# A written-out job order for an attention and MLP kernel, replaced by another with four changes of tiling fewer

## The chip, the cores and the metric

The kernel runs on one core of a Trainium2 chip. The time is that of one launch on the device, in microseconds (us); the median over several runs is given. A core has TensorE (PE, the matrix unit, whose weight loads the profile shows apart as PEld), VectorE (DVE), ScalarE (ACT), GpSimd (POOL) and SyncE (SP, which here only issues transfers). Each of them works through its own queue in order, and they wait for each other through semaphores. Matmuls write to PSUM, which has eight banks of 128 x 512 floats.

## The reference

One input x of 2048 tokens by 512 features is normalized once, and two branches are added to it:

```python
xn  = layernorm(x)
out = x + A(xn) + B(xn)
# A: attention, 32 heads of 16, in 4 segments of 512 tokens one after the other:
#    logits = q k^T * scale + mask (causal), p = softmax(logits), a_dot = p v
#    a_mem  = phi(q) M / (phi(q) z + 1e-6)      M, z: memory of the earlier segments
#    o      = g * a_mem + (1 - g) * a_dot       g = sigmoid(beta), one for each head
#    M += phi(k)^T v,  z += sum of phi(k);  phi(t) = t + 1 if t > 0 else exp(t)
#    A = concat(o) wo
# B: gelu(layernorm(xn) w1 + b1) w2 + b2       512 -> 1792 -> 512
```

## The kernel before, in words

The work is cut into 1308 jobs, and the order of the jobs is written out by hand as a string (ORDER, line 98), one letter a job. A letter names one of 39 streams (line 58); each stream is a list of jobs in a fixed order of its own, and the letter takes the next one of its stream. The function plan (line 130) walks through the string, and the kernel's last loop (line 896) calls the function of each job, which puts its instructions on the queues of all engines at once. So the string sets the order of every engine's queue and of the transfers too: on each engine the instructions stand in the order of the jobs, and an instruction waits until the data that it reads and the buffer that it writes are free. A second string (BANKS, line 115) gives the PSUM bank of each accumulation tile in the order in which they are asked for (line 160).

Matrix products of 512-long sums are made with float16 halves: each operand is a high and a low part, and three products are added (split3, line 483). Weights are therefore loaded, squared and summed for a scale, scaled and split in the kernel itself.

The attention works in 16 groups i = 4 s + g, segment s (512 tokens) and head group g (8 heads). The jobs that matter here, with the letters of the string:

- a: X, load, statistics and scaling of 256 tokens, and Xt, their transposition. b: ratio. f: zeros and constants. u: warm, eight matmuls without use that fill the start.
- g and h: T(i, 1) for keys and T(i, 0) for queries (line 515): twelve matmuls, a copy by ScalarE and one by VectorE, three writes to device memory on SP's queue (lines 528 to 530), and, when both of a group are there, four reads that bring them back in another layout as kst and qst (line 536).
- i: N, the transposed keys. j: M(i, n), the maximum over the logits, n from 0 to 11, two or four matmuls with an eviction by VectorE each (lines 638 and 645), and R(i), which turns the maxima, sends them through memory and adds them to qst (lines 651 to 661).
- k: S(i, t, n), logits and exponentials (lines 678 and 683) and GpSimd's selects (line 692). l: pv and PV, the sums over values (line 707). m: O, normalization. n: K, the memory's update (line 619), and Z, Qd and Q, its use. o: V(s, b), the values (line 604), copied by ScalarE (line 610).
- p: D(j, f), the first MLP product for 256 tokens and half of the 1792 columns, seven in a set (line 771). q: G and H, gelu and the split. r: e(j, n), the second MLP product, six matmuls each, fourteen in a set (line 814). s: out, the product with wo (line 832). t: A(tok, 0), the load of x into an accumulator tile by SP (line 793), and A(tok, 1), the add of b2 to it by a transfer that GpSimd issues (line 797).
- v to D: the weights' loads (wl), and E to M: their squares (wm), scales (wf) and splits (ws). "1a" and "1b" are the first and second half of w1, "2a" and "2b" those of w2; qk, QK and RK are the head groups 0, 1 and 2 with 3 of wk and wq. The squares of 1a are made by TensorE (line 315), those of 1b by ScalarE (line 308), and wf adds them up by matmuls with ones (lines 349 and 351).

TensorE's array is used in three tilings: whole (T, V, D, out, warm and the weights' sums), in two halves of 64 rows (e, M, S, R, N, Qd and the later transpositions), and in four strips of 32 columns (pv, PV, K). Where two jobs that follow each other differ in it, the tiling changes. ScalarE changes its function table for gelu and back, 16 times each.

## Time and profile before

| what | value |
|---|---|
| median of 3 runs | 695.29 us (694.94 to 695.43) |
| profiled execution, its own time | 700.17 us |
| span of the profile | 698.5 us |
| TensorE busy | 684.0 us |
| VectorE, ScalarE, GpSimd busy | 542.7, 503.8, 340.4 us |
| granted TensorE clock, mean | 0.995 |

The profile shows one execution. Its span runs from the first to the last recorded instruction; the execution's own time is 1.7 us longer. A row of the timeline merges instructions of one line that follow each other: start, busy time, engine and line, what it writes and reads, its shape and how many. The busy time of a matmul reaches to its modelled end, so rows overlap, and the distance between starts tells the work better. In brackets stands idle time before the row and what ended it. A row of the waits gives who waited for whom, the sum in us, how often, and the longest. A row of the windows gives the busy time of the engines in a stretch, and behind them TensorE's granted clock, the share of the DMA engines that was busy, and GB/s. A row of the DMA issues names what is moved, the queue, how many and KB each.

### The profile page before, as it was taken

To read this page: it belongs to the slowest core of one execution; us is meant where nothing else is said; L and a number is where in the kernel's file an instruction comes from. 1 tells how busy PE (TensorE), PEld (TensorE's weight loads), DVE (VectorE), ACT (ScalarE), POOL (GpSimd) and SP (SyncE) were. 2 spreads that over 40 slices of the span, in tenths; PEclk is the share of its full clock that TensorE was granted. 3 is DMA by queue.
4 is the path that set the end of the run, shared out by engine and by line. 5 is a ranking of instruction groups with operands and counts; after the bars stand their busy time and mean duration, and the time that the engine had idled before them with its cause. 6 is when DMAs were issued, how large, how long until landed. Compare 5 with 4: busy or idle time off the path is not lost.

```text
span 698.5 us, 17165 instructions
## 1 busy us (share of the span) xinstructions
PE 684.0 (98%) x6465; PEld 396.0 (57%) x6465; DVE 542.7 (78%) x1740; ACT 503.8 (72%) x972; POOL 340.4 (49%) x526
## 2 busy tenths in 40 slices
PE   8999999999999999989999999999999999999997
PEld 6754656565644556555554556567464456556543
DVE  5988967997877967878687787988768588969432
ACT  4466898798786669647884787766876586877970
POOL 5235567365532634535324455355444335565752
PEclk9999999999999999999999999999999999999999
DMA  9986022411404131412123223051130404140101
GB/s 261 290 247 170 18 60 66 107 48 26 115 3 122 47 81 44 96 43 62 40 55 92 92 71 99 8 117 31 24 87 25 130 17 137 33 106 2 20 1 60
DMA packets 51791, 55.13 MB, mean 79 GB/s; under 512 B 4782, under 2 KB 40636, under 8 KB 51708
## 3 DMA queue, kind: packets, MB, share of 16 engines
q1 hardware_dynamic: 49404, 49.84, 24.8%
q0 software_dynamic: 2304, 4.20, 3.6%
q8 instruction: 50, 0.82, 0.5%
q14 instruction: 33, 0.27, 0.1%
HBM read 36.99 MB, written 17.04 MB: 77 GB/s over the span
## 4 chain that ended last, share of the span: by engine, by line
PE 84%; DMA 7%; ACT 3%; DVE 2%; SPq 1%; issue 1%; POOL 0%; DVEq 0%; ACTq 0%
PE ps L489 33%; PE ps L814 20%; PE ps L707 9%; PE ps L832 6%; PE ps L678 5%; PE ps L638 5%; DMA qd<-hl 2%; DMA qst<-qd 2%; PE ps L580 1%; PE ps L508 1%; DMA w1s<-in_B_w_dram 1%; ACT pt L683 1%; DMA oT<-in_B_w_dram 1%; DMA wqs<-in_A_wq_dram 1%; PE ps L845 1%
## 5 line engine op out<-in xcount | busy, mean ns | idle before, releaser
L645 DVE CUSTOM_DVE_ANT_0 ps<-ps,mask 128x512 f32<-128x512 f32 (+3 forms) x512 | 234.7, 523 | 17.6 <-PE ps L638 14.9
L683 ACT ACTIVATE pt<-ps,qkcs 128x512 f32<-128x512 f32 (+1 forms) x384 | 208.3, 621 | 52.9 <-PE ps L678 49.3
L814 PE MATMUL ps<-w2s,hT 64*128 64x512 f16 x1344 | 175.8, 377 | 0.6 <-DVE acc L820 0.5
L489 PE MATMUL ps<-xnT,w1s 128*128 128x256 f16 x1344 | 158.4, 273 | 0.0
L692 POOL TENSOR_SCALAR_AFFINE_SELECT pt<-pt 128x256 f32<-128x256 f32 x256 | 101.2, 415 | 95.2 <-ACT pt L683 93.9
L489 PEld LDWEIGHTS <-w1s 128*128 128x128 f16 x1344 | 127.7, 98 | 29.0 <-issue 11.0
L789 POOL TENSOR_TENSOR hT<-hh,hT 128x512 f16<-128x512 f32 x64 | 68.1, 1064 | 94.5 <-ACT hT L788 94.5
L814 PEld LDWEIGHTS <-hT 64*128 64x128 f16 x1344 | 71.7, 94 | 54.9 <-issue 4.5
L707 PE MATMUL ps<-pt,vt 128*32 128x512 f32 (+3 forms) x1024 | 76.0, 435 | 0.1
L773 DVE SCALAR_TENSOR_TENSOR hT<-ps,sc,sr 128x256 f32<-128x256 f32 x112 | 51.9, 478 | 27.2 <-PE ps L489 26.6
L645 DVE DVE_READ_ACCUMULATOR2_ANT mc<- 128x1 f32 x512 | 71.6, 140 | 0.1
L638 PE MATMUL ps<-kst,qst 48*128 48x512 f16 (+3 forms) x512 | 66.6, 298 | 2.9 <-DMA qst<-qd 2.3
L678 PE MATMUL ps<-qst,kst 50*128 50x512 f16 (+3 forms) x512 | 66.6, 298 | 1.8 <-DMA qst<-md 0.9
L788 ACT ACTIVATE hT<-hh 128x512 f16<-128x512 f32 x64 | 36.6, 573 | 27.7 <-POOL hh L787 27.2
L707 PEld LDWEIGHTS ps<-pt,vt 128*32 128x32 f32 x1024 | 31.1, 109 | 41.2 <-issue 32.2
L787 POOL TENSOR_SCALAR hh<-hT,sc 128x512 f32<-128x512 f32 x64 | 42.0, 656 | 23.1 <-ACT hT L780 20.8
L780 ACT ACTIVATE hT<-hT,b1t 128x256 f32<-128x256 f32 x112 | 46.7, 495 | 2.0 <-DVE hT L773 1.8
L489 PE MATMUL ps<-wvs,xnT 128*128 128x512 f16 x192 | 45.7, 390 | 0.0
L737 POOL TENSOR_TENSOR nN<-nN,oT 128x512 f32<-128x512 f32 x16 | 20.3, 1267 | 51.2 <-DVE oT L555 51.2
L678 PEld LDWEIGHTS <-kst 50*128 50x128 f16 x512 | 27.1, 94 | 31.2 <-issue 14.5
L489 PE MATMUL ps<-xnT,wqs 128*128 128x512 f16 x192 | 44.2, 380 | 0.0
L638 PEld LDWEIGHTS <-qst 48*128 48x128 f16 x512 | 28.1, 95 | 28.4 <-issue 9.3
(225 smaller groups left out, 909.9 us busy)
## 6 DMA issues: line engine op xcount, KB each, us to landing
kd<-hl SPq DMA_DIRECT2D x48, 128.0 KB
qd<-hl SPq DMA_DIRECT2D x48, 128.0 KB
kst<-kd SPq DMA_DIRECT2D x32, 192.0 KB
qst<-qd SPq DMA_DIRECT2D x32, 192.0 KB
acc<-in_A_x_dram SPq DMA_DIRECT2D x16, 256.0 KB
acc<-in_B_b_dram POOLq DMA_DIRECT2D x16, 256.0 KB, 4.1
out_dram<-acc SPq DMA_DIRECT2D x16, 256.0 KB
xt<-in_A_x_dram SPq DMA_DIRECT2D x14, 256.0 KB
```

What stands on the lines that cost most here:

```text
L489: T.matmul(p, wsl(ws, k, a), xsl(xs, k, b), start=s0 and i == 0, stop=s1 and i == 3 * n - 1)
L638: T.matmul(p[:, o:o + n], stk[i, 0][r, t, P * qb:P * qb + P], stk[i, 1][r, t, :n], start=True, stop=True)
L645: V.tensor_tensor_reduce(p[:, o:o + n], p[:, o:o + n], mask[:, 512 - n:], 1.0, -3e38, OP.add, OP.max, mc[:, 16 * b + 4 * t + qb:16 * b + 4 ...
L678: T.matmul(p[:, o:o + n], stk[i, 1][r, t, P * kb:P * kb + P], stk[i, 0][r, t, P * kb:], start=True, stop=True)
L683: A.activation(e[:, OFF[kbs[0]]:OFF[kbs[0]] + o], p[:, :o], AF.Exp, scale=qkcs[:, 1, i % NG:i % NG + 1])
L692: G.affine_select(v, v, pattern=[[0, 2], [1, P]], compare_op=OP.is_ge, fill=0.0, base=0, channel_multiplier=-1)
L707: T.matmul(p[32 * c:32 * c + 32, P * kb:], vt[s, kb][:, 4 * g + c, 16 * odd:16 * odd + 32], pt[i, 2 * c + odd][:, OFF[kb]:OFF[kb] + LEN[kb ...
L773: V.scalar_tensor_tensor(hz[:, fi, :], p[:, :256], col(F1 + fh), srow[hs][:, own], op0=OP.mult, op1=OP.mult)
L780: A.activation(z, z, AF.Gelu_apprx_tanh, bias=b1t[:, FH * (j % 2) + f:FH * (j % 2) + f + 1])
L787: G.tensor_scalar(t, hz[:, z, :], col(SHH + j % 2), 0.0, op0=OP.mult, op1=OP.add)
L789: G.tensor_tensor(hT[:, z, 1, :], t, hT[:, z, 0, :], op=OP.subtract)
L814: w = T.matmul(pes[j][a], hTs[fh][r, fi, u, P * a:P * a + P], w2s[r, fo, v, :], start=n == 0 and m == 0, stop=fi == FH - 1 and m == 2, ski ...
```

## The change

All code stays. The two strings are replaced: ORDER has the same letters in another order, so that the streams' own orders stand, and BANKS has other banks to fit. By its description the new order makes 225 changes of tiling in place of 229 and is one that allows for late loads and for GpSimd's transfers beside the queue's.

```diff
 ORDER = (
-    "auauvfdcauufaExauuEaGxaGwEbyfaFFGyEaEGGuAzuFzegHHJHauFGJuGHiAHHhCHFIIBtHpHHppHIJppIpJpBjjqBJIIgjIqjtoKCIIoujqjK"
-    "jKKhKIJojqLqjoLjrjjrrrnJKLDrDjijKrjppKMLKJLtkJrkpkjrkjrjKJrkpkjpKjMLjllllpKkjtrjkpkjkrjLrLkLkgjnlLlLqltluhqppkL"
...
+    "aufauucvafauaxuEdwuxEGayFEbayuFGEaaGuAeGzEzFGguHHGJHufFiHAHHhHIJIHpHpJHGIpHJFIppppIjjIBqjBqBgIJKoItIqKKoKujjjCC"
+    "hIKLjqjjLoLoDJKjajrrjnKrrqLrjijtrJjpKpKJLJkrkkpkjrKjrtjkpJpkjrtjKKjltlllpjkrLjkpkjkrjrLLkkgjLllLntqllhppqLrkLDk"
...
 )
 BANKS = (
-    "012531714607252301476502431056712645213076407541623037541231607543273410265734012654012654061254065421065421056"
...
+    "307127514306527014705325621740356523475160172345670124345762013561047235612043715620415642015625401642501654201"
...
 )
```

What this does at the places of which the prediction speaks:

- Start. Before, warm jobs 8 and 9 both stand behind the squares of 1a; now warm 8 stands ahead of them. The loads of v's second part and of QK change places.
- Second halves of w1 and w2. Before, the loads were issued in the order 2b first part, 1b first part, A(0, 0), 1b second and third part, T(1, 1)'s writes, 2b second part. Now it is the three parts of 1b, T(1, 1)'s writes, A(0, 0), and both parts of 2b. The squares of 1b stand before or around V(0, 1) instead of from V(0, 0) to T(1, 0); its wf job stays behind T(1, 0). The load of the next tokens (X(1, 0, 0)) moves from the start to M(0, 9).
- Group 7, from T(7, 0) to M(7, 0), jobs in order. Before: H e e e e M A(6, 1) e M M e G e M e H e M D D R M(7, 0). Now: e H e G e M e e e M e H M e e M M D H D R(6) A(6, 0) e M(7, 0), and A(6, 1) follows later, ahead of the first S of group 6.
- Group 15. Before: A(15, 0) PV M(15, 0) M(15, 1). Now: PV M(15, 0) S M(15, 1), and A(15, 0) later.
- Group 13. The last e job of set 11 now stands before T(14, 1) instead of behind it, and Z(14) before S(13, 0, 1).
- V(1, 3) moves from ahead of D(5, 0) to four short jobs ahead of K(4).
- A(tok, 0) and A(tok, 1) of most tiles change places against the other jobs; for tiles 9, 11 and 12 the two now stand close together.

## The prediction

> **What bounds the kernel now.** I read the page first, then the chain of work that ended last, then TensorE's own waits, and then the timeline of TensorE and of the queues around each of those waits.

> ```profile
> span 698.5 us, 17165 instructions
> PE 684.0 (98%) x6465; PEld 396.0 (57%) x6465; DVE 542.7 (78%) x1740; ACT 503.8 (72%) x972; POOL 340.4 (49%) x526
> ```

> TensorE is busy for 684.0 of 698.5 us, so it sets the time, and since the change adds and removes no matmul, only three things can move the end: the changes of tiling, the 14.5 us in which TensorE is idle, and stretches in which it is busy at a lower clock. In the timeline (columns: start us, busy us, engine and instruction, then in brackets the idle time before it and what ended it) the work of one job is the distance from its start to the next job's start:

> ```profile
> 104.50 0.81 PE L814 MATMUL ps<-w2s,hT 64*128 64x512 f16 x6
> 105.24 4.11 PE L489 MATMUL ps<-xnT,w1s 128*128 128x256 f16 x36
> 109.28 0.72 PE L678 MATMUL ps<-qst,kst 50*128 50x256 f16 x8
> ...
> 112.78 0.38 PE L638 MATMUL ps<-kst,qst 48*128 48x512 f16 x2
> 113.00 1.46 PE L814 MATMUL ps<-w2s,hT 64*128 64x512 f16 x12
> 114.29 0.49 PE L638 MATMUL ps<-kst,qst 48*128 48x384 f16 x6
> ```

> Two e jobs followed by a job of their own tiling (113.00 to 114.29) take 1.29 us, 0.645 each; one e followed by a D job, which uses the whole array, takes 0.74. A change of tiling is thus worth about 0.095 us. Three D jobs and one change take 4.04, so a D is (4.04 - 0.095) / 3 = 1.315. An M job of two matmuls takes 0.22.

> The two costliest places are these. The first is the scale of the second half of w1 (the wf job of "1b", lines 349 and 351) and the V job behind it; the first two rows show the same kind of job undisturbed, with six matmuls instead of ten, the windows show TensorE's granted clock as the third number from the right:

> ```profile
> 24.81 0.50 PE L349 MATMUL ps<-am,ones 128*128 128x1 f32 x4
> ...
> 25.47 0.46 PE L508 MATMUL ps<-ident,phk 64*128 64x64 f32 x8
> ...
> 53.46 0.28 PE L349 MATMUL ps<-am,ones 128*128 128x1 f32 x2
> 54.52 0.38 PE L349 MATMUL ps<-am,ones 128*128 128x1 f32 x2 [0.78 <-ACT w1s L308]
> ...
> 56.50 4.44 PE L489 MATMUL ps<-wvs,xnT 128*128 128x512 f16 x12
> ...
> 61.30 2.76 PE L489 MATMUL ps<-wvs,xnT 128*128 128x512 f16 x12
> ```

> ```profile
> 57.00:61.00 4.00, 4.00 (x13) 1.43 (x13) 2.28 (x8) 0.20 (x2) 0.00 (x0) 0.59 0.61 173
> 300.00:310.00 10.00, 8.40 (x61) 4.03 (x62) 6.40 (x25) 4.80 (x9) 2.27 (x2) 0.83 0.07 22
> ```

> Six such matmuls take 0.66 undisturbed, so ten would take 1.1; they took 56.50 - 53.46 = 3.04. That is 1.9 us of waiting, and then the V job takes 4.44 instead of 2.76, because the clock stood at 0.59: 1.7 us more. The second place is the first M job of head group 7:

> ```profile
> 292.28 0.58 SPq L530 DMA_DIRECT2D qd<-hl  x1
> 292.43 0.88 POOL L797 DMA_DIRECT2D acc<-in_B_b_dram  x1
> ...
> 297.70 1.25 SPq L536 DMA_DIRECT2D qst<-qd  x2
> ...
> 299.53 0.26 PE L508 MATMUL ps<-ident,mc 64*96 64x64 f32 x2
> 301.49 0.89 PE L638 MATMUL ps<-kst,qst 48*128 48x512 f16 x2 [1.70 <-DMA qst<-qd]
> ```

> TensorE stands still from about 299.6 to 301.49, 1.9 us, and the window 300 to 310 then has a mean clock of 0.83: 17% of 10 us, 1.7 us. So an idle gap here is paid about twice.

> **The change part by part.** Nothing but two strings changes: the order of the jobs on all engines, and the PSUM banks that go with it. I decoded both orders by the streams function and added up, with the prices above, the TensorE work that stands between each producer and its consumer (its cover).

> Tilings: by the shapes of the tiles I count 227 and 223, four fewer as stated, and by net count three of the four are steps from a row-tiled to a whole-array job, like the e and D above: 4 x 0.095 = 0.4 us. All of it is on the path, since TensorE is the path. Bounds 0.2 to 0.5.

> Start: one warm-up job is moved from behind the squares of w1's first half to just ahead of them.

> ```profile
> 21.16 1.61 PE L315 MATMUL ps<-w1s 128*128 128x128 bf16 x25 [0.79 <-DMA w1s<-in_B_w_dram]
> ...
> 22.84 1.03 PE L845 MATMUL ps<-ones 128*128 128x256 f16 x8
> 23.71 0.39 PE L315 MATMUL ps<-pt 128*128 128x128 bf16 x4
> ```

> A warm-up takes 23.71 - 22.84 = 0.87, and it now fills the 0.79 us in which TensorE waited for that load, which other loads of the same total size precede as before. Gain 0.8, bounds 0 (if an earlier stage of the start is late instead; the squares of the second q and k group now stand nearer to their load) and 0.9.

> Second half of w1: its squares on ScalarE waited for the load.

> ```profile
> 50.24 1.48 ACT L308 ACTIVATE w1s<-w1s 128x1536 bf16<-128x1536 f32 x1 [2.79 <-DMA w1s<-in_B_w_dram]
> ...
> 35.74 0.45 SPq L276 DMA_DIRECT2D w2s<-in_B_w_dram  x1
> 36.23 1.38 SPq L273 DMA_DIRECT2D w1s<-in_B_w_dram  x2
> 37.65 3.70 SPq L793 DMA_DIRECT2D acc<-in_A_x_dram  x1
> 41.40 3.88 SPq L273 DMA_DIRECT2D w1s<-in_B_w_dram  x2
> ```

> ```profile
> w2s<-in_B_w_dram SPq DMA_DIRECT2D x1, 1280.0 KB
> w1s<-in_B_w_dram SPq DMA_DIRECT2D x4, 320.0 KB
> ```

> On SP's queue 1280 KB of w2 and an acc tile stand ahead of or between these loads; in the new order both stand behind all of them. The 1280 KB are as much as the four w1 loads together, and the issues at 37.65 and 41.40 take 3.7 and 3.9 us, which tells of a full queue. From 35.7 to 50.2 some 2.8 MB moved, 5 us per MB: without the 1.5 MB the load lands several us earlier. The squares also stand about 3 us earlier in ScalarE's order. I take the whole wait and the slow clock as gone: 1.9 + 1.7 = 3.6, bounds 0 and 3.6.

> Group 7: in the order before, the add of b2 (line 797, issued by GpSimd) falls on the write and read of group 7's queries; in the new order it comes behind the first M. What remains is shown by group 14, with no such transfer:

> ```profile
> 584.44 0.57 SPq L530 DMA_DIRECT2D qd<-hl  x1
> ...
> 587.91 0.79 SPq L536 DMA_DIRECT2D qst<-qd  x2
> ...
> 592.09 0.69 PE L638 MATMUL ps<-kst,qst 48*128 48x512 f16 x6
> ```

> There 3.5 us pass from the last write's issue to the read's, against 5.4 in group 7, and 7.65 to the first M. Added to 292.28 this gives 299.9, where TensorE was at 299.6. The new order also has one e job more between the projection and the first M (ten for nine; five M, two D and R as before): 0.645 us. The cover grows so from 9.7 to 10.3 (nine e 5.8, five M 0.9, two D 2.6, changes and R 0.4), and the smallest over all groups from 8.8 to 10.0. The wait goes, and the slow clock with it: 1.9 + 1.7 = 3.6, bounds 0 and 3.9.

> [...]

> Two smaller waits:

> ```profile
> 587.30 0.70 PE L678 MATMUL ps<-qst,kst 50*128 50x256 f16 x7 [0.84 <-DVE hT L773]
> ...
> 628.88 0.55 PE L638 MATMUL ps<-kst,qst 48*128 48x512 f16 x4 [0.63 <-DMA qst<-qd]
> ```

> The jobs around the first are regrouped (the e pair's two evictions on VectorE come earlier); around the second an S job now stands between the first and second M, 0.2 us. I take 0.5 off for each, bounds 0 and 0.8, 0 and 1.3.

> What becomes thinner: the last V of the second segment stands 0.6 us before the K job that reads it (6.9 before), and ScalarE must copy it in between:

> ```profile
> 60.97 0.60 ACT L610 ACTIVATE vt<-ps 128x512 f32<-128x512 f32 x1 [3.80 <-PE ps L489]
> ```

> With 0.60 for the copy K, and with it all of TensorE's queue, waits 0.1 if ScalarE is free, 1 to 2 if it is behind. V to K of group 0 falls from 3.3 to 2.0, and M to R of groups 0 and 15 to some 2.4. The covers of the banks are alike in both orders. Three adds of b2 (tiles 9, 11, 12) now stand within 1 us of the load that they need, and GpSimd waits there with its selects for the S jobs queued behind it; the one such wait before was 0.9 us:

> ```profile
> POOL acc L797 <- DMA acc<-in_A_x_dram: 0.9, 1, 0.9
> ```

> The smallest cover from such an S to its reader is 1.6 us in both orders. With what I can't see I put 2.0 on this, bounds 0 and 6.

> Sum on the profiled execution: -0.4 - 0.8 - 3.6 - 3.6 - 1.0 + 2.0 = -7.4. Its own time is 700.17 and the median of the runs 695.29, 4.9 less with the same work, so some of the waits must be smaller when nothing is recorded. Idle 14.5 plus 3.4 of slow clock is 17.9; if the 4.9 lies there, 13/17.9 = 0.73 remains. Then the gain is 0.4 + 0.73 x 7.0 = 5.5, and the median 695.3 - 5.5 = 689.8. All good bounds and no new wait: 0.4 + 0.73 x 10.9 = 8.4, or unscaled 11.4.

> **The rivals.** (1) The waits removed belong to the recorded execution alone: the 4.9 us between profile and median are just these. Then 0.4 and the start are left and the thinner covers take them back: 694.8, no change. For it speaks that the two dips and gaps sum to 7.2; against it, that the load order and the 9.7 us of cover in group 7 are there in every run. (2) The clock dips come by themselves: 689.8 + 0.73 x 3.4 = 692.3. The two dips right behind the two longest waits speak against it. [...] (3) The collision moves: GpSimd's add now falls between R of group 6 and its first S, whose cover is 4.9 us by the count; a wait like group 7's of 1.9, with the clock, takes 3.6 x 0.73 = 2.6 back: 692.4. (4) Slower: the second half of w2 is now loaded last, behind group 1's keys, and its squares stand in ScalarE's order ahead of the copies of V that K of group 0 needs. At 5 us per MB its 2 MB take 10 us from about 45 and land near 55, ScalarE gets there at about 53. Beyond 2 us of lateness (the cover of V to K) each us is TensorE's, and from 1.5 us of gap on the clock adds 1.7. If the load takes 10 us longer than this, 8 + 1.7 us come on top of 689.8: 699.5. It decides against the change from some 6 us on. For it speaks that issues on SP took up to 3.9 us in this stage; against it, that less is queued then.

> **How the numbers follow.** A measurement of this kernel can tell about 0.2%, 1.4 us, from no change: 693.9 and 696.7 are the bounds. The forecast, 689.8, has 0.52; rival 1 has 0.14, rival 2 0.08, rival 3 0.12, rival 4 0.14. Faster by over 0.2%: 0.52 + 0.08 + 0.12 = 0.72. Within: 0.14. Slower: 0.14. The range runs from 685.0 (between the scaled and unscaled good ends, 686.9 and 683.9) to 695.0 (rival 1); left out are rival 4 and a few in a hundred below.

> **What would show it.** In the changed profile: no idle before line 349 at the second half of w1, the V job behind it 2.8 long and a clock of 1.0 to 65 us (load step); group 7's first M without a wait for qst, the write to read distance near 3.5 (collision step); the squares of w1's first half without the wait (start). The forecast is wrong if TensorE's idle time and slow clock stay near 17.9 in total, if a wait of over 1.5 us appears at K of group 0, S of group 6 or elsewhere, or if the median moves while these stay.

## The result, and the profile after

| what | before | after |
|---|---|---|
| median | 695.36 us (694.94 to 697.78, 4 runs) | 688.95 us (687.50 to 690.04, 4 runs) |
| profiled execution, its own time | 700.17 us | 688.33 us |
| span, granted clock | 698.5 us, 0.995 | 686.6 us, 0.999 |

The ratio is 0.9899 with a 95% interval of 0.9869 to 0.9930: the new order is faster by 6.4 us. The forecast was 689.8. Between the two profiled executions lie 11.8 us, where the prediction's sum was 7.4. Single executions, in three of the kernels' sets, took 1,390 to 1,770 us; they are left out, and as the only profile of e6 is of one of them, nothing is read from it.

The first lines of the page after:

```profile
span 686.6 us, 17170 instructions
PE 678.2 (99%) x6465; PEld 389.3 (57%) x6465; DVE 542.9 (79%) x1740; ACT 502.3 (73%) x972; POOL 338.5 (49%) x526
```

TensorE is idle for 686.6 - 678.2 = 8.4 us instead of 14.5, and its busy time, with the same 6465 matmuls, is 5.8 less. That can be matmuls at a higher clock, fewer changes of tiling, or short waits that were counted as busy. TensorE's own waits of after (who, for whom, sum in us, how often, longest):

```profile
PE ps L845 <- POOL ones L167: 1.6, 1, 1.6
PE ps L638 <- DMA qst<-qd: 0.7, 2, 0.5
PE ps L678 <- ACT pt L683: 0.5, 1, 0.5
PE ps L315 <- DMA wks<-in_A_wk_dram: 0.3, 1, 0.3
PE ps L678 <- DMA qst<-md: 0.2, 1, 0.2
```

And four of before's:

```profile
PE ps L349 <- ACT w1s L308: 1.5, 3, 0.8
PE ps L678 <- DMA qst<-md: 0.9, 1, 0.9
PE ps L315 <- DMA w1s<-in_B_w_dram: 0.8, 1, 0.8
PE ps L814 <- DVE acc L820: 0.5, 1, 0.5
```

The 1.6 at line 845 is the very start of the kernel and stood there before. Line 349 is gone from the list, line 315 no longer waits for w1, and the longest wait for qst is 0.5.

**Start and w1.** TensorE in the timeline of after, at the squares of w1's first half and at the scale of its second half:

```profile
19.09 1.04 PE L845 MATMUL ps<-ones 128*128 128x256 f16 x8
19.96 2.05 PE L315 MATMUL ps<-w1s 128*128 128x128 bf16 x28
...
51.47 0.95 PE L349 MATMUL ps<-am,ones 128*128 128x1 f32 x8
52.28 0.36 PE L351 MATMUL ps<-am,ones 128*128 128x1 f32 x2
52.58 0.72 PE L638 MATMUL ps<-kst,qst 48*128 48x512 f16 x8
53.23 5.35 PE L489 MATMUL ps<-wvs,xnT 128*128 128x512 f16 x24
```

The warm-up stands ahead of the squares, which start without a wait. The wf job takes 52.58 - 51.47 = 1.11, the 1.1 that the prediction worked out for it undisturbed, and the two V jobs behind it take 5.35, where one alone took 4.44 before: no slow clock. The windows that showed the two slow stretches before:

```profile
57.00:61.00 4.00, 4.00 (x60) 1.85 (x58) 3.52 (x12) 3.33 (x8) 3.24 (x5) 1.00 0.71 173
300.00:310.00 10.00, 9.91 (x106) 6.64 (x106) 9.96 (x34) 8.18 (x17) 5.81 (x11) 1.00 0.17 31
```

The clock, third number from the right, was 0.59 and 0.83 and is now 1.00. Why the squares are in time stands in SP's and ScalarE's rows of after:

```profile
33.88 2.56 SPq L273 DMA_DIRECT2D w1s<-in_B_w_dram  x4
36.49 2.18 SPq L266 DMA_DIRECT2D acc<-in_B_w_dram  x2
...
45.36 0.46 SPq L793 DMA_DIRECT2D acc<-in_A_x_dram  x1
45.86 0.43 SPq L276 DMA_DIRECT2D w2s<-in_B_w_dram  x1
```

```profile
44.56 1.48 ACT L308 ACTIVATE w1s<-w1s 128x1536 bf16<-128x1536 f32 x1 [0.25 <-issue]
```

All of the second half of w1 is issued by 38.7, the acc tile and w2 only from 45.4. ScalarE makes the first square at 44.56 instead of 50.24, and no longer waits for the load.

**Group 7.** SP's transfers of the queries, and TensorE at R(6), an e job and M(7, 0):

```profile
288.03 0.57 SPq L530 DMA_DIRECT2D qd<-hl  x1
...
291.68 0.79 SPq L536 DMA_DIRECT2D qst<-qd  x2
```

```profile
295.24 0.26 PE L508 MATMUL ps<-ident,mc 64*96 64x64 f32 x2
295.34 0.81 PE L814 MATMUL ps<-w2s,hT 64*128 64x512 f16 x6
295.99 0.38 PE L638 MATMUL ps<-kst,qst 48*128 48x512 f16 x2
```

From the last write to the read are 3.65 us instead of 5.42, and M(7, 0) starts 7.96 us after the write without a wait (9.21 before).

**Where the 11.8 us came from.** I laid the jobs of each order on the trace and summed, stretch by stretch, the time from a job's start to the next one's beyond what that job takes undisturbed, changes of tiling included. This is TensorE's lost time, waits and slow clock together, in us:

| up to | before | after | e1 | e2 | e3 | e4 | what lies there |
|---|---|---|---|---|---|---|---|
| T(0,0) | 3.9 | 2.4 | 3.5 | 3.8 | 3.1 | 3.1 | start |
| V(0,3) | 3.6 | -0.2 | -0.1 | 0.6 | -0.1 | -0.1 | second half of w1 |
| T(6,0) | 1.1 | 2.8 | 1.6 | 1.1 | 2.4 | 3.4 | groups 0 to 5 |
| T(8,0) | 5.3 | 0.7 | 3.4 | 1.6 | 1.6 | 1.5 | group 7 |
| T(12,0) | 1.8 | 2.2 | 2.5 | 3.0 | 2.6 | 1.9 | |
| end | 6.8 | 3.2 | 6.4 | 6.8 | 6.2 | 4.5 | groups 12 to 15 |

Start 1.5, w1 3.8 and group 7 4.6 were gained, groups 0 to 5 lost 1.7, the last groups gained 3.6. With 0.4 for four changes of tiling and 0.4 lost in the middle this is the 11.8. Each column is one execution: e3 and e4 have the same jobs up to T(12, 0) and still differ by 1.0 in groups 0 to 5.

### The profile page after: what moved, and what is told of

Read it like the earlier page. It is cut to its first block, busy times and chain, and to the rows that moved or that the text cites. A ratio compares the mean times of both kernels' runs of the same rounds, so it can differ in the third digit from the quotient of the medians.

```text
span 686.6 us, 17170 instructions
## 1 busy us (share of the span) xinstructions
PE 678.2 (99%) x6465; PEld 389.3 (57%) x6465; DVE 542.9 (79%) x1740; ACT 502.3 (73%) x972; POOL 338.5 (49%) x526
## 4 chain that ended last, share of the span: by engine, by line
PE 82%; DMA 7%; ACT 4%; DVE 4%; issue 1%; SPq 1%; POOL 0%; ACTq 0%; DVEq 0%
PE ps L489 34%; PE ps L814 18%; PE ps L707 9%; PE ps L832 6%; PE ps L678 5%; PE ps L638 5%; DVE ps L645 2%; ACT pt L683 2%; DMA qst<-qd 2%; DMA qd<-hl 1%; PE ps L580 1%; DMA w1s<-in_B_w_dram 1%; PE ps L508 1%; DMA wvs<-in_A_wv_dram 1%; PE ps L315 1%
## 5 line engine op out<-in xcount | busy, mean ns | idle before, releaser
L814 PE MATMUL ps<-w2s,hT 64*128 64x512 f16 x1344 | 173.8, 375 | 0.1
L489 PE MATMUL ps<-xnT,w1s 128*128 128x256 f16 x1344 | 157.7, 273 | 0.3
L489 PEld LDWEIGHTS <-w1s 128*128 128x128 f16 x1344 | 127.9, 98 | 28.3 <-issue 10.2
L814 PEld LDWEIGHTS <-hT 64*128 64x128 f16 x1344 | 68.5, 94 | 56.2 <-issue 2.9
L773 DVE SCALAR_TENSOR_TENSOR hT<-ps,sc,sr 128x256 f32<-128x256 f32 x112 | 51.9, 478 | 26.0 <-PE ps L489 25.0
L638 PE MATMUL ps<-kst,qst 48*128 48x256 f16 (+3 forms) x512 | 64.4, 297 | 0.8 <-DMA qst<-qd 0.7
L678 PE MATMUL ps<-qst,kst 50*128 50x512 f16 (+3 forms) x512 | 64.1, 298 | 0.8 <-ACT pt L683 0.5
L489 PE MATMUL ps<-xnT,wqs 128*128 128x512 f16 x192 | 44.2, 380 | 0.0
L489 PE MATMUL ps<-xnT,wks 128*128 128x512 f16 x192 | 44.1, 379 | 0.0
L489 PE MATMUL ps<-wvs,xnT 128*128 128x512 f16 x192 | 43.8, 379 | 0.1
L832 PE MATMUL ps<-wos,oT 128*128 128x512 f16 x192 | 43.2, 379 | 0.0
```

The lines of the kernel that those rows point to most:

```text
L489: T.matmul(p, wsl(ws, k, a), xsl(xs, k, b), start=s0 and i == 0, stop=s1 and i == 3 * n - 1)
L638: T.matmul(p[:, o:o + n], stk[i, 0][r, t, P * qb:P * qb + P], stk[i, 1][r, t, :n], start=True, stop=True)
L678: T.matmul(p[:, o:o + n], stk[i, 1][r, t, P * kb:P * kb + P], stk[i, 0][r, t, P * kb:], start=True, stop=True)
L773: V.scalar_tensor_tensor(hz[:, fi, :], p[:, :256], col(F1 + fh), srow[hs][:, own], op0=OP.mult, op1=OP.mult)
L814: w = T.matmul(pes[j][a], hTs[fh][r, fi, u, P * a:P * a + P], w2s[r, fo, v, :], start=n == 0 and m == 0, stop=fi == FH - 1 and m == 2, ski ...
L832: T.matmul(p, o[:, u, P * b:P * b + P], wos[:, g, v, :], start=i == 0, stop=i == 3 * NG - 1)
```

## A counter that the runs had: dips of the clock

Each execution comes with its mean granted clock. In the profile of before the granted clock is 0.50 from 56.83 to 60.24 us and from 302.59 to 306.00, and 1.00 between. One such dip of 3.41 us is half a per cent of the span, so it takes about 0.0025 off the mean, and the values fall into three groups: 0.999 and above, 0.997 to 0.998, 0.996 and below. The unchanged kernel, in the three groups of runs beside the experiments:

| | no dip | one | two |
|---|---|---|---|
| e0 to e3 | 11, median 695.76 | 12, 697.71 | 6, 699.76 |
| e4 to e7 | 18, 695.48 | 10, 697.70 | 6, 698.19 |
| e8 to e11 | 12, 695.29 | 6, 697.61 | 4, 700.91 |

By these medians the executions with one dip take 1.95 to 2.32 us more than those without. The profiled execution of before, 700.17 at 0.995, had both; the runs at 694.94 to 695.43 have the time of executions without any (their clocks weren't listed). For each experiment the table gives the ratio to before, in how many executions the clock dipped, and the median of those in which it didn't, less that of before in the same group:

| kernel | ratio, 95% interval | with a dip | without dips, us | against before |
|---|---|---|---|---|
| e0_before | 1.0015, 0.9993 to 1.0037 | 9 of 12 | 694.75 | -1.0 |
| e1_loads | 0.9985, 0.9968 to 1.0002 | 1 of 11 | 696.16 | +0.4 |
| e2_add | 0.9948, 0.9930 to 0.9965 | 0 of 5 | 693.90 | -1.9 |
| e3_both | 0.9957, 0.9942 to 0.9972 | 2 of 11 | 694.22 | -1.5 |
| e4_tail | 0.9944, 0.9923 to 0.9965 | 5 of 12 | 692.29 | -3.2 |
| e5_start | 0.9960, 0.9938 to 0.9982 | 2 of 12 | 694.25 | -1.2 |
| e6_tilings | 1.0088, 1.0061 to 1.0114 | 2 of 8 | 703.22 | +7.7 |
| e7_gap | 0.9953, 0.9931 to 0.9975 | 5 of 10 | 692.97 | -2.5 |
| e8_tilings | 1.0001, 0.9977 to 1.0026 | 0 of 10 | 696.78 | +1.5 |
| e9_undo | 0.9924, 0.9899 to 0.9950 | 4 of 12 | 690.71 | -4.6 |
| e10_better | 0.9898, 0.9867 to 0.9929 | 0 of 6 | 689.25 | -6.0 |
| e11_after | 0.9908, 0.9875 to 0.9941 | 1 of 6 | 689.75 | -5.5 |

The last column holds to about 1 us: e0 is the unchanged kernel, and its three executions without a dip stand at -1.0.

## The experiments

In the diffs a line is a job, and only the jobs around an edit are shown.

**e0_before**: nothing changed.

> The kernel before, unchanged, against itself. The profiled execution of before took 700.17 us and the median of its runs 695.3. Theory: the two waits (second half of w1, first M of group 7) and the two dips of the clock behind them are in most executions, in varying size: the ratio is 1.00, and executions with a mean granted clock of 0.995 (two dips of 3.4 us at half clock) are longer by 1.7 us for each dip than those with 1.0. Rival 1 of the prediction (the waits belong to the recorded execution alone): the timed executions show a clock of 1.0 throughout, and a new profile shows the two waits again all the same.

Measured 698.17. Its profile (699.29, one dip) has the wait before line 349 as well (1.7 in sum), and 1.1 at M(7, 0) without a dip behind it. Both waits are there in more than one execution; the dips come and go.

**e1_loads**: w2's load and A(0, 0) go behind those of w1 in the order before.

```diff
 T(0,0)
-wl 2b first part
 ws 1a
...
 wl 1b first part
-A(0,0)
...
-A(0,1)
 V(0,0)
 wm 1b
+A(0,0)
+wl 2b first part
 wl 2b second part
...
 M(1,0)
+A(0,1)
```

> Before, with one edit: the first load of the second half of w2 and the first accumulator load (with its add) stand behind all loads of the second half of w1. Theory: the squares of w1's second half no longer wait, the wait of 1.9 us and the slow clock of 1.7 us behind it go, so the profile loses about 3.6 us against the one of before and the median 2.6 (1.9 to 3.6). Rival 1: no change in the median. Rival 4: the second half of w2 is late in its place, a wait of over 1.5 us appears at K of group 0 or at the scale of w2's second half, and the gain is given back.

Measured 696.17, ratio 0.9985 (0.9968 to 1.0002). TensorE's rows of e1 at the scale of w1's second half:

```profile
53.04 0.95 PE L349 MATMUL ps<-am,ones 128*128 128x1 f32 x8
...
54.07 2.75 PE L489 MATMUL ps<-wvs,xnT 128*128 128x512 f16 x12
```

The wait and the slow V job are gone, so the load order was their cause. In time it brings about 1.0 us (0.15%), where 2.6 were expected, and the interval reaches to no change. What there is comes from the dips, 1 execution of 11 instead of 18 of 29; executions without a dip are no shorter (+0.4, within that column's 1 us). Group 7 still waits in it (SP's and TensorE's rows of e1):

```profile
288.66 0.58 SPq L530 DMA_DIRECT2D qd<-hl  x1
...
293.92 1.15 SPq L536 DMA_DIRECT2D qst<-qd  x2
```

```profile
297.23 0.39 PE L638 MATMUL ps<-kst,qst 48*128 48x512 f16 x1 [1.07 <-DMA qst<-qd]
298.03 0.39 PE L638 MATMUL ps<-kst,qst 48*128 48x512 f16 x1 [0.41 <-DMA qst<-qd]
```

**e2_add**: GpSimd's add of tile 6 goes behind M(7, 0) in the order before.

```diff
 M(6,7)
-A(6,1)
 e(5,4)
...
 O(5,2)
+A(6,1)
```

> Before, with one edit: GpSimd's add of b2 to tile 6 stands behind the first M of group 7 instead of ahead of it. Theory: the time from the write of group 7's queries to their read falls from 5.4 to about 3.5 us, the wait of 1.9 falls to some 0.3 (the cover is still 9.7 us) and the dip of the clock goes: profile 3.3 us less than before, median 2.4 (1.7 to 3.6) less. Rival 1: no change in the median. Rival (the write is slow by chance, not by GpSimd's transfer): the distance stays near 5 us.

Measured 693.90, ratio 0.9948 (0.9930 to 0.9965). SP's and TensorE's rows of e2 for the same jobs:

```profile
289.23 0.58 SPq L530 DMA_DIRECT2D qd<-hl  x1
...
292.92 0.79 SPq L536 DMA_DIRECT2D qst<-qd  x2
```

```profile
296.49 0.26 PE L508 MATMUL ps<-ident,mc 64*96 64x64 f32 x2
296.58 0.66 PE L638 MATMUL ps<-kst,qst 48*128 48x512 f16 x2
```

Against e1, which has the add in its old place, the write to the read is 3.69 for 5.26 us, and M(7, 0) follows R without a pause 7.35 us after the write, where it came 8.57 after it in e1 and 9.21 in before. One transfer moved, and the wait is gone; in e3, e4 and e5, which have the same move, M(7, 0) follows R without a pause as well, and in before, e0 and e1 it waits 1.1 to 1.9. The collision is shown. It is worth 1.9 us without any dip (e3, with e1's edit too, has 1.5). Its profile waits only 0.37 at w1, in the same order as before; why it waits so much less there isn't known.

**e3_both**: both edits.

> Before, with both edits (loads and add). Theory: the gains add up, about 5 us in the median (3.6 to 7), most of what the whole change brought (6.4), with none of the other some hundred moves. Rival (the gain is in the many small moves): the two edits together bring less than half of it, under 3 us.

Measured 694.59, ratio 0.9957 (0.9942 to 0.9972): no more than e2 alone, and 3.0 us by the ratio, so under half of the whole change, as the rival has it. The profile tells what came in place (TensorE at the scale of w2's second half):

```profile
68.00 0.73 PE L349 MATMUL ps<-am,ones 128*128 128x1 f32 x6
69.57 0.38 PE L349 MATMUL ps<-am,ones 128*128 128x1 f32 x2 [0.84 <-ACT w2s L308]
```

Now the second half of w2 is late, by 0.8: rival 4's cause at another place, since its squares hold back its own scale and not ScalarE's copies of V. In after this place loses 0.25.

**e4_tail**: e3, and from job 1028 on (behind M(12, 11), the last M of group 12) the new order.

```diff
 jobs 1 to 1027 as in e3
-jobs 1028 to 1308 of the order before
+jobs 1028 to 1308 of the new order
```

> Before with the two edits (loads, add) up to job 1027 (the last M of group 12, some 520 us in), and the new order from there on. Theory: the regroupings of groups 13 to 15 (waits of S(13, 2, 0) 1.0, M(15, 2) 0.8, S(15, 0, 0) and e(14, 0) 1.7 us in the kernel with both edits, of which the profile of after shows some 1.2) bring 2.0 to 2.8 us: 0.3 to 0.4% below the kernel with both edits, about 0.9925 of before. Rival (those waits move with chance, not with the order): no difference to the kernel with both edits (0.9957).

Measured 693.04, ratio 0.9944 (0.9923 to 0.9965); without dips 3.2 under before, where e3 was 1.5 under. The expectation had 0.9925. Its profile loses 1.7 us less than e3's from T(12, 0) to the end, and there the profiles part by the order: 6.2 to 6.8 us are lost in the six of the old tail (e0 and e5 have 6.3 and 6.4), 3.2 to 4.5 in the five of the new one (after, e4, and e7, e9 and e11 with 3.2 to 4.1). The regrouped tail is a gain of its own, larger than the 1.0 put down for it.

A closer look at group 15 shows where a part is from. SP's rows of before and of after for R(15), which sends the maxima to memory (L658) and reads them back (L661), and what TensorE waited for:

```profile
645.74 0.30 SPq L658 DMA_DIRECT2D md<-mhl  x1
648.77 0.53 SPq L661 DMA_DIRECT2D qst<-md  x2
```

```profile
650.37 0.89 PE L678 MATMUL ps<-qst,kst 50*128 50x512 f16 x5 [0.92 <-DMA qst<-md]
...
654.10 0.82 PE L814 MATMUL ps<-w2s,hT 64*128 64x512 f16 x6 [0.52 <-DVE acc L820]
```

```profile
634.95 0.30 SPq L658 DMA_DIRECT2D md<-mhl  x1
636.35 0.53 SPq L661 DMA_DIRECT2D qst<-md  x2
```

The read can be issued 3.03 us after the write before, 1.40 after. No transfer of GpSimd is near. In the stretch 645.7 to 648.8 of before the page of the DMA queues has only these:

```profile
q1 hardware_dynamic: 80, 0.02, 2.7%
q8 instruction: 1, 0.02, 1.9%
```

A packet of the queue called instruction moves with the 16 KB of the write, in the same 0.15 us (183 GB/s in that slice). In after and in e4 such a packet comes in a slice of its own, 0.3 us behind, and the read follows 1.40 and 1.39 us after the write. The distance is 2.83 to 3.31 in before, e0, e1, e2, e3, e5 and e9, and 1.39 to 1.40 in e4, e7, e8, e10, e11 and after. In before the packet starts 0.99 us behind the write's issue, among the write's own packets, the last of which starts at 2.05; in after it starts 1.19 us behind, when the last of the write's own has started at 1.03. That the packet causes it is read from this pattern alone; no run moved it by itself. The order doesn't decide it alone: e9 has the new tail and 3.29, and loses 0.9 more there than e11.

**e5_start**: the new order up to job 345 (e(2, 8)), then e2's.

```diff
-jobs 1 to 345 of the order before
+jobs 1 to 345 of the new order
 jobs 346 to 1308 as in e2
```

> The new order up to job 345 (150 us in: start, weights, first segment), and from there on the order before with GpSimd's add moved behind the first M of group 7. Theory: against the kernel with both edits it has the moved warm-up and the loads of the start as well, worth 0.8 us (0.5 to 1.5): about 0.9945 of before; no waits of over 1 us in the first 70 us but the cold first warm-ups. Rival: no difference to the kernel with both edits.

Measured 694.55, ratio 0.9960 (0.9938 to 0.9982). Up to V(0, 3) its profile loses 2.2 us less than e2's (2.43 - 0.22 against 3.82 + 0.56), but from there to T(6, 0) 1.2 more, and the time is no better than e2's or e3's, as the rival has it (the profiled execution, 692.13, is the shortest of its twelve). In the profile the thinner covers of groups 0 to 5 give back about half of the better start.

**e6_tilings and e8_tilings**: after, with jobs of two tilings exchanged, 28 times in e6 (279 changes for 223 by the shapes) and 15 times in e8 (253). One of e8's:

```diff
 D(13,5)
 O(12,2)
+S(13,2,2)
 D(13,6)
-S(13,2,2)
```

> After, with 28 pairs of neighbouring jobs exchanged, so that 279 tilings change in place of 223 by the same count (56 more); nothing else is added. Theory: 56 x 0.095 = 5.3 us more than after (4.5 to 6.5 with side effects on waits): about 694.5, by which the four changes less of the change are worth 0.4. Rival (a change of tiling is hidden behind the weight loads): under 2 us more. Rival (it costs more than the rows show): over 8.

> After, with only 15 exchanges, each an M or S job (none of them waits for a transfer) moved ahead of the D job before it: 253 changes of tiling for 223, 30 more; the D that is passed is 0.1 to 0.3 us later, nothing else. Theory: 30 x 0.095 = 2.9 us above after (2.4 to 4), with the same waits as after in the profile; the 14 us of the kernel with 56 more then came from waits that its exchanges made, since there S and M jobs came 1.3 us later. Rival (a change of tiling costs some 0.25 us): 7.5 us above after, with distances between the starts of a D and the S behind it that show it.

Measured: e6 703.72, some 13 above after for 56 changes, where 56 x 0.095 is 5.3. e8 696.78, 7.0 above e11 for 30 changes, where the price is 2.9. TensorE at that place in e8:

```profile
583.74 2.79 PE L489 MATMUL ps<-xnT,w1s 128*128 128x256 f16 x24
587.77 0.28 PE L678 MATMUL ps<-qst,kst 50*128 50x256 f16 x2 [1.23 <-DVE hT L773]
587.99 1.49 PE L489 MATMUL ps<-xnT,w1s 128*128 128x256 f16 x12
```

The S job stands between two D jobs, and its bank is still being emptied by VectorE, which is behind with the D before: 1.23 us of waiting. Summed over the trace, e8 loses 4.5 us more than e11 beside its changes of tiling, in waits of this kind, and 30 x 0.095 + 4.5 = 7.4 against 7.0 measured. The price itself can be read from the starts: over the thirteen profiles (all but e6's) a D job takes 1.31 us in the median ahead of a job of its own tiling and 1.41 ahead of an M or S, an M job of two matmuls 0.22 and 0.31. So the 0.095 holds, and the expectation that an exchange costs nothing else is wrong. e6 is of the same kind, but its terms were not separated.

**e7_gap**: after, with T(7, 0) later and M(7, 0) earlier, to make a gap on purpose.

```diff
-T(7,0)
 e(5,0)
 H(5,3)
 e(5,1)
+T(7,0)
...
+M(7,0)
 e(5,9)
-M(7,0)
```

> After, with the query projection of group 7 two e jobs later and one e job behind the first M in place of ahead of it: the cover from projection to first M falls from 10.3 to 8.4 us, against 9.9 needed. Theory: TensorE stands still 1.5 us (1 to 2) before the first M of group 7, and the clock then falls to half for 3.4 us in most executions, so the time is 1.5 + 1.7 = 3.2 us above after. [...]

Measured 693.99, ratio 0.9953 (0.9931 to 0.9975). The wait came at another place than meant (TensorE's rows):

```profile
285.50 1.47 PE L814 MATMUL ps<-w2s,hT 64*128 64x512 f16 x12 [2.32 <-DVE ame L589]
...
298.83 0.89 PE L638 MATMUL ps<-kst,qst 48*128 48x512 f16 x2
```

Without T(7, 0) ahead of it, e(5, 0) waits 2.32 us, and M(7, 0) hardly does. Without dips it is 3.2 us above e11, the size that was expected, but from another wait: that is luck. The executions answer another question: the same order had a dip in 5 of 10, 694.75 against 692.97, 1.8 us. In the profiled one the gap of 2.32 was followed by none. So with this gap a dip came in some executions, not in all (the last section sets it beside the grid of the clock); after, without the gap, had one in 1 of 6 (e11).

**e9_undo**: after, with the loads of w2 and A(0, 0), A(6, 0) and A(6, 1) put back.

```diff
+wl 2b first part
 wl 1b first part
+A(0,0)
...
-A(0,0)
...
-wl 2b first part
 wl 2b second part
...
+A(6,0)
 T(7,0)
...
 M(6,7)
+A(6,1)
...
 R(6)
-A(6,0)
...
 O(5,2)
-A(6,1)
```

> After, with the two named steps undone: the first load of the second half of w2 and the first accumulator load stand ahead of the loads of w1's second half again, and both transfers of tile 6 stand where they stood before, ahead of the first M of group 7. Theory: both waits come back, the first with about 1 to 2 us, the second with 0.5 to 1.3 (the cover is 10.3 and not 9.7), and with them dips of the clock in a good part of the executions: 2.5 to 5 us above after. Rival (the rest of the new order makes these two steps needless): under 1 us above after.

Measured 690.98, ratio 0.9924 (0.9899 to 0.9950), 1.2 above e11 (1.0 without dips). That is less than expected. A dip came in 4 executions of 12 against 1 of 6, too few to tell apart. TensorE's rows of e9, at w1, and at an e job and M(7, 0):

```profile
50.08 0.27 PE L638 MATMUL ps<-kst,qst 48*128 48x256 f16 x1 [0.97 <-ACT vt L610]
...
54.10 0.38 PE L349 MATMUL ps<-am,ones 128*128 128x1 f32 x2 [0.47 <-ACT w1s L308]
...
297.62 0.81 PE L814 MATMUL ps<-w2s,hT 64*128 64x512 f16 x6
298.27 0.91 PE L638 MATMUL ps<-kst,qst 48*128 48x512 f16 x2
```

The wait at w1 is back, for the most part at another place: ScalarE's first square waits 3.48 us for the load, the copy of V behind it on ScalarE comes late, and TensorE waits 0.97 for that copy, besides the 0.47 at line 349. Up to V(0, 3) e9 loses 2.2 us more than e11, so the new order does not cover this load order. At M(7, 0) only 0.3 is back. The add was issued 0.82 us behind the last write, not 0.15 as in before, and the write to the read took 3.52, so the collision itself hardly came back, and what the new order's e job ahead of M(7, 0) is worth against it is not shown. The profile is 2.2 us longer than e11's; why the medians are only 1.2 apart isn't known.

**e10_better and e11_after**: after with three jobs moved against waits that its profile still shows, and after itself.

```diff
 e(0,4)
+e(0,5)
 R(0)
...
 T(11,1)
-A(10,0)
...
 T(11,0)
+A(10,0)
...
 e(13,11)
+e(13,12)
 S(15,0,2)
```

> After, with three moves more: the load of tile 10 behind group 11's transfers instead of ahead of R of group 10 on SP's queue (in the profile of after the maxima's write took 3.7 us there, group 11's writes stood behind it, and the first M of group 11 waited 0.7), one e job ahead of S(15, 0, 2) (0.6 of waiting for ScalarE), one e job ahead of R(0) (0.3). Theory: these waits go, 1.0 to 1.6 us below after in the profile, 0.2% in the median. Rival (other waits take their place): no difference to after.

> After, unchanged, on the same chip and beside the same runs of the kernel before as the three others. Theory: 0.990 of before, and no execution, or one in ten, with a dip of the clock, where before has one or two dips in half of its executions or more. Rival (the dips come by themselves): dips as often as before.

Measured 689.24 (ratio 0.9898, 0.9867 to 0.9929) and 689.78 (0.9908, 0.9875 to 0.9941): no difference that can be told. In the profile of e10 the wait for acc's load behind T(11, 0) shrinks, but 1.1 us stand at M(15, 0) and the job behind it, and 0.5 ahead of e(14, 0).

## Why the prediction was right, and where not

- **Tilings, -0.4.** The price holds (see e8); four changes alone are below what the runs can tell.
- **Start, -0.8.** Direction right, under-sized: 1.5 between the profiles. The 0.8 at line 315 for w1 went as said; the wait for wk (0.8 before, 0.3 after) wasn't counted, and it varies (0.2 in e0, 0.5 in e3). e5 shows that a gain here is partly given back up to T(6, 0).
- **Second half of w1, -3.6.** Right in the profile, -3.8, and its cause is shown by e1. That the issues of 3.7 and 3.9 us tell of a full queue was the author's reading and isn't shown; in after the same load of x into acc is issued in 0.46. But executions of e1 without a dip were no shorter than before's, so in the median it wasn't there in this size; e9 has it back with 2.2 in the profile.
- **Group 7, -3.6.** Right in its cause (e1 against e2), -4.6 in its stretch: the jobs right behind the gap lost 1.7 us to the slow clock (3.41 us at 0.50), and a wait of 0.3 behind S(7, 2, 1) went as well.
- **Two smaller waits, -1.0.** This step failed in size: groups 12 to 15 gave 3.6. S(13, 2, 0) gave 0.7 and the M jobs of group 15 0.8, which is near the 1.0. Not counted were two waits that stood in TensorE's waits of before: 0.9 for qst<-md and 0.5 for acc, at S(15, 0, 0) and e(14, 0), now 0.65 together instead of 1.77. The last 1.0 of the 3.6 lies in small pieces. The prediction looked at what the edits named and not at the whole list.
- **Thinner covers, +2.0.** Measured +1.7 in groups 0 to 5, in many places: 0.3 at R(0) as foreseen for M to R, 0.25 at w2's scale, 0.3 at M(1, 10). The 0.3 foreseen at R(15) came too, in the last stretch. No wait at K of group 0.
- **The sum, -7.4**, was short of the profile's -11.8 by these. Its good end counts the tilings twice: 10.9 has the 0.4 in it, so 8.4 and 11.4 should be 8.1 and 10.9. The forecast doesn't hang on it.
- **The scaling by 0.73.** This step failed in its reason. The 4.9 us between profile and median were laid on all waits alike. The executions show that they are mostly two dips of the clock (2.7, 4.0 and 5.6 us in the three groups of runs), which the median run, by its time, hadn't. So the 3.4 us of slow clock were not there to be gained in a median of such runs, while the waits were not all smaller by a quarter: group 7's was there in full without dips (e2, 1.9), w1's not to be seen (e1). Without the dips the prediction's sum is -7.4 + 3.4 = -4.0, or 691.3; executions without dips gave -5.5 (e11) and the first runs -6.4. The uncounted waits and the wrongly counted clock nearly cancelled, and that 689.8 came out so close to 688.95 is luck. The two steps that make 7.2 of the sum brought 3.0 us in the order before (e3, by the ratio) and cost 1.2 when undone in the new one (e9): the mechanisms were right, their weight in the median wasn't.

Of the rivals, (1) is half true: the dips belong to some executions, while the collision's wait is in every profile of the old order with the add in its old place (before, e0, e1), and the time moved without dips too. (2) is wrong as put: after had a dip in 1 of 6 executions, before in 10 of 22 beside it, and e7, which has a gap, in 5 of 10. (3) didn't happen: the window from 300 to 310 us has TensorE busy for 9.91 of 10. (4) appears in small, 0.25 us in after and 0.8 to 1.4 in e3 and e4, far from the 6 us at which it would decide. Of its terms, the 5 us per MB counted only some of the loads: from 35.7 to 50.2 us of before 3.92 MB moved, 3.7 us per MB. That a gap of 1.5 us is enough for a dip was an estimate from the two of before; e7's gap of 2.32 had none behind it.

What stays open: the share of each of the many small moves in the middle, why the wait at w1 shows in the profiles and not in the time of executions without a dip, and why S(15, 0, 2) still waits 0.5 us for ScalarE.

## What to carry to other kernels

When a profiled execution and the median differ, first sort the executions by their granted clock: what only the recorded one shows is not there to be gained. A transfer that another queue started together with a write and its read-back made the first use here come 1.2 to 1.9 us later (e1 and before against e2), so look at what is issued within some tenths of a us of each such write, the queue called instruction too. And cost every wait in the list, not those alone that the edit names: in a kernel that is 98% busy with its bound, many waits of 0.3 to 1 us make up the result, and a new order that saves some of them makes others.

## What the runs showed of the hardware that was not expected

```profile
299.18:302.59 3.41, 1.60 (x13) 0.65 (x13) 1.91 (x9) 2.74 (x6) 1.85 (x2) 1.00 0.35 94
...
281.09:284.51 3.42, 2.09 (x16) 0.97 (x14) 3.35 (x10) 0.69 (x1) 2.22 (x3) 1.00 0.36 115
```

  The grid lies differently in the executions: counted from the span's start, a step begins at 2.22 us in before, at 2.59 in after and, by its row, at 1.20 in e7. That could be why the same order has 0, 1 or 2 dips (before), or one in 5 of 10 (e7). It isn't shown: the executions without a profile can't be looked into, and two dips are few.
- **A small write and the read behind it took twice as long beside one other packet.** R's write of 16 KB and the read behind it took 1.39 to 1.46 us from issue to issue in the 14 groups of before and after in which nothing else moved, and 2.97 and 3.03 in groups 4 and 15 of before, where the only other traffic was one packet of 16 KB on the queue called instruction, 0.94 and 0.99 us behind the write's issue. In group 15 of after the same packet came 1.19 us behind, and it took 1.40.
- **The add doesn't always lengthen the write.** With the add issued 0.15 us behind the last write, the write to the read took 5.42 in before and 5.26 in e1, but 3.73 in e0, where the read's data came late instead and M(7, 0) waited 1.1 all the same. In e9, with the add 0.82 us behind, it took 3.52. The time from the last write to M(7, 0), 8.6 to 9.2 with the add 0.15 us behind and 7.4 without it (e2), is the safer number.
